# Sharing PSUM banks, splitting the first loads, and turning x by DMA in a fused attention and SoLU kernel

## The chip, the cores and the metric

The kernel runs on one core of a Trainium2 chip. The core has a matrix engine (TensorE, in the profile PE, with its weight loads shown apart as PEld), a vector engine (VectorE, DVE), a scalar engine (ScalarE, ACT), a general engine (GpSimd, POOL) and a queue engine (SyncE, SP) that here only issues DMAs. Matrix products are written to PSUM, which has eight banks of 2 KB in each of 128 partitions; VectorE and ScalarE read them from there. The metric is the device time of one execution in microseconds, lower is better.

## The reference, cut to what matters

Sizes: 4 batches, 8 heads, 768 tokens, head dimension 64; then 3072 tokens of 512 features through a layer with 1024 hidden units. Inputs and output are float32.

```python
scores = scale * q @ k.T                      # per batch and head, 768 x 768
keep = (key < 8) | ((0 <= query - key) & (query - key < 96))
scores = where(keep, scores - slope[head] * dist, -1e9)
x = softmax(scores) @ v                       # heads side by side: 3072 x 512
h = x @ w_in                                  # 3072 x 1024
solu = h * softmax(h)                         # over the 1024 units
ln = (solu - mean) / sqrt(var + 1e-6) * g_ln
out = ln @ w_out                              # 3072 x 512
```

Each query needs only the 95 keys before it, itself, and the 8 global keys. So a tile of 128 queries meets two blocks of 128 keys (one for the first tile of a batch).

## The kernel before, in words

Tokens go in 24 tiles of 128, six to a batch; tile n belongs to batch n // 6. The work of the whole program is a set of small tasks, and the names in brackets are those of the planner.

Once per batch, for each of four pairs of heads and for q and for k (eight units): load 384 KB (ql, tile `raw`, ten buffers), cast to 16 bits (qc, `qkn`, four buffers; POOL, in batch 0 also DVE), six transposes on PE into PSUM (qt, `pt`), copy to SBUF in token order (qo, `qkT`; ACT or DVE).

Once per tile: load v (vl, `vst`, four buffers), cast it on POOL (vc, into `vo`); in two halves of four heads: scores on PE (s, `ps`), exponential on ACT (e, `eb`), multiplication by the mask and bias on DVE (m), product with v on PE (av, `pav`). POOL copies the global keys and values to where the next tile finds them (gk, gv). DVE divides by the sum (n, `x16`), PE turns x with four transposes (xt, into another `pt`), DVE copies it out (xc, `xT`). Then the layer: h on PE, eight matmuls of 512 columns (h, `ph`), exponential on ACT (he, `e`), product on DVE (u, `u`), a DMA transpose of u issued by SP (ut, `uT`), squares on ACT (q), statistics on POOL or DVE (st, pw), eight matmuls into the output (o, `po`), scaling on ACT or DVE (os, `osb`), store (w).

Once in all: `w_in` is loaded by a DMA that POOL issues (L443); `w_out` in four loads; each of its eight blocks is scaled by g (gr, L453 and L456), PE forms their mean (gm, `pm`, L463), and DVE subtracts it (gc, eight instructions, L467). The first `po` needs all eight.

All PSUM pools hold one buffer each: `ps` two banks, `pav` two, `ph` two, `pt` one (for both kinds of transposes), `po` one (and `pm` once). So a step that writes `ph` waits until the product u of the tile before has been read out of it.

The order on every engine is fixed when the program is built. A list scheduler (class Plan) takes one task after the other; among the tasks that could start at about the same time on an engine it takes the one with the smallest due time, T * (n + DUE[what] + i * DUE[what+]), with two numbers per task kind from the table DUE. Its costs serve only to order the work. Every DMA except the load of w_in goes through SP's queue, in one order, and SP waits at each transposition or store until its source is ready; what stands behind waits too.

Of the kernel before, what the change touches and what calls it, by code (L numbers as in the profile page):

```python
# [100 lines left out]
def kernel(  # L101
# [24 lines left out]
    T = 4.34  # L126
    LAG = 7


    DUE = {  # L130
# [32 lines left out]
    with tc.manual_schedule():  # L163
# [35 lines left out]
        for h in range(H):  # L199
# [18 lines left out]
            rooms={"s": 1, "av": 1, "t": 1, "h": 1, "o": 1, "vst": 4, "raw": 10,  # L218
                   "qkn": 4, "eb": 4, "x16": 2, "xT": 3, "e": 3, "u": 5, "ut": 5, "uT": LAG + 1,
# [20 lines left out]

        raws, qkn, pts, qkT = {}, {}, {}, {}

        def load_pair(b, w, pr):
            t = sb.tile([P, 2, NA * D], FP32, name="raw", bufs=10)
            nc.sync.dma_start(  # L245
                out=t, in_=(q, k)[w][b, 2 * pr : 2 * pr + 2].rearrange(
                    "m (p a) d -> p m (a d)", a=NA))
            raws[b, w, pr] = t

        def cast_pair(b, w, pr, eng):  # L250
            t = sb.tile([P, NA, 2, D], FP16, name="qkn", bufs=4)
            ENG[eng](out=t.rearrange("p a m d -> p m a d"),  # L252
                     in_=raws.pop((b, w, pr)).rearrange("p m (a d) -> p m a d", d=D))
            qkn[b, w, pr] = t

        def turn_pair(b, w, pr):
            pt = pts[b, w, pr] = psum.tile([P, NA, P], FP16, name="pt", tag="t")
            src = qkn.pop((b, w, pr))
            for a in range(NA):
                nc.tensor.transpose(  # L260
                    out=pt[:, a, :], in_=src[:, a].rearrange("p m d -> p (m d)"),
                    identity=ident)

        def order_pair(b, w, pr, eng):
            if b not in qkT:
                qkT[b] = sb.tile([P, 2 * NP, S], FP16, name="qkT")
            dst = qkT[b][:, w * NP + pr, :].rearrange("p (t a) -> p t a", a=NA)
            ENG[eng](out=dst, in_=pts.pop((b, w, pr)).rearrange("p a t -> p t a"))  # L268
# [9 lines left out]
        def scores(n, half):  # L278
            b, a = divmod(n, NA)
            nb = 2 if a else 1  # L280
            ps = pss[n, half] = psum.tile([P, 2, 2, 2, P], FP32, name="ps", tag="s")
# [50 lines left out]
        def norm(n):  # L332
# [4 lines left out]
            x16 = sb.tile([P, 2, 4, D], FP16, name="x16")  # L337
# [5 lines left out]
        def turn_x(n):  # L343
            x16 = x16s.pop(n).rearrange("p g i d -> p (g i d)")
            pt = xps[n] = psum.tile([P, NCC, P], FP16, name="pt", tag="t")
            for c in range(NCC):
                nc.tensor.transpose(out=pt[:, c, :], in_=x16[:, ts(c, P)], identity=ident)  # L347

        def copy_x(n, eng):
            xTs[n] = sb.tile([P, NCC, P], FP16, name="xT", bufs=3)  # L350
            ENG[eng](out=xTs[n], in_=xps.pop(n))
# [62 lines left out]
        def ffn_out(n):  # L414
            uT = uTs.pop(n)
            po = pos[n] = psum.tile([P, D_MODEL], FP32, name="po", tag="o")
            for c in range(NFC):
                nc.tensor.matmul(out=po, lhsT=uT[:, c, :], rhs=gw_sb[:, c, :],  # L418
# [4 lines left out]
        def scale_out(n, eng):  # L423
            osb = osbs[n] = sb.tile([P, D_MODEL], FP32, name="osb", bufs=3)
            g, i = place[n]
            rs = rss[g][:, i : i + 1]
            if eng == sc:
                nc.scalar.activation(out=osb, in_=pos.pop(n), func=AF.Copy, scale=rs)  # L428
            else:
                nc.vector.tensor_scalar(out=osb, in0=pos.pop(n), scalar1=rs,  # L430
                                        scalar2=None, op0=ALU.mult)

        def store(n):
            nc.sync.dma_start(out=out[ts(n, P), :], in_=osbs.pop(n))
# [25 lines left out]
        def gw_mean():  # L460
            pms.append(psum.tile([P, D_MODEL], FP32, name="pm", tag="o"))
# [10 lines left out]
        def due(what, n, i=0):  # L472

            return T * (n + DUE[what] + i * DUE.get(what + "+", 0.0))

# [4 lines left out]
        for b in range(B):  # L480
            for i, (w, pr) in enumerate(PAIRS):
                x = (b, w, pr)
                k_ = str(min(b, 2))
                for what, engs, emit, kw in (
                    ("ql", {"SP": 0.5}, lambda e, x=x: load_pair(*x),
                     dict(takes=("raw",), load=1.08)),
                    ("qc", {gp: 0.86, ve: 0.6} if b == 0 else {gp: 0.86},
                     lambda e, x=x: cast_pair(*x, e),
# [111 lines left out]
```

## Time and profile before

| | us |
|---|---|
| median of 3 runs | 170.19 (169.99 to 170.49) |
| the profiled execution's own time | 169.84 |
| its span on the core | 168.1 |
| ACT busy | 127.3 (76%) |
| DVE busy | 118.4 (70%) |
| POOL busy | 73.8 (44%) |
| moved by DMA | 34.85 MB, 207 GB/s over the span |

The span runs from the first to the last instruction that the profiler saw on the core; 1.74 us of the execution's own time lie outside it. A row of the timeline gives start, length, engine, line of the kernel, operation, output and inputs; in brackets how long the engine had been idle and what released it. A row of the chain of waits gives start, length and what the end hung on there. In the stages (windows) each engine has its busy time in that stretch, and "DMA share" is the mean share of the 16 DMA engines that had a packet under way, which may pass 1 where packets overlap.

### The profile page before, as it was taken

The numbers are of one execution on the slowest core, as the hardware profiler recorded it, in microseconds if no ns is written. First come the engines' busy times: TensorE is split into PE (matmuls) and PEld (weight loads), VectorE is DVE, ScalarE is ACT, GpSimd is POOL, SyncE is SP. The second block draws the span as 40 slices with busy tenths as digits, with TensorE's granted clock in tenths as the row PEclk, the third lists the DMA queues.
The fourth block names the chain that finished last, engine by engine and source line by source line (L and its number), as shares of the span: only waits on it lengthen the run. The fifth ranks groups of instructions, "written<-read, shape, count | busy, mean of one in ns | idle before, by whom it ended". The sixth has DMA issues, their size and how long they took to land.

```text
span 168.1 us, 3666 instructions
## 1 busy us (share of the span) xinstructions
PE 142.3 (85%) x1384; PEld 78.7 (47%) x1384; DVE 118.4 (70%) x221; ACT 127.3 (76%) x201; POOL 73.8 (44%) x154
## 2 busy tenths in 40 slices
PE   0346479878799999999999999999999999998670
PEld 0334253455465565555545455555454555543220
DVE  1355066799998968887898778987899888744300
ACT  3955585988898978999878887879787977667511
POOL 6410116576983878636775475730404133011100
PEclk9999999999999999999999999999999999999998
DMA  5999999499999999999999999834534336545841
GB/s 177 314 314 209 349 322 346 97 278 281 189 263 312 264 359 219 226 272 226 245 304 268 260 210 257 185 96 125 127 80 113 96 95 125 125 125 125 95 161 62
DMA packets 65138, 34.85 MB, mean 207 GB/s; under 512 B 52320, under 2 KB 60512, under 8 KB 65120
## 3 DMA queue, kind: packets, MB, share of 16 engines
q1 hardware_dynamic: 64592, 33.57, 81.4%
q0 software_dynamic: 528, 1.05, 3.3%
q8 instruction: 11, 0.18, 0.5%
q14 instruction: 7, 0.06, 0.1%
HBM read 23.07 MB, written 6.29 MB: 175 GB/s over the span
## 4 chain that ended last, share of the span: by engine, by line
PE 44%; DMA 26%; SPq 16%; POOL 6%; issue 4%; DVE 2%; ACT 1%; POOLq 0%; ACTq 0%
PE ph L361 16%; PE po L418 14%; DMA raw<-in_k_dram 10%; DMA vst<-in_v_dram 6%; SPq L229 6%; SPq L245 6%; PE ps L287 5%; DMA uT<-u 5%; PE pav L325 5%; DMA raw<-in_q_dram 4%; SPq L447 3%; POOL qkn L252 3%; PE pt L260 2%; PE pt L347 2%; POOL vo L234 2%
## 5 line engine op out<-in xcount | busy, mean ns | idle before, releaser
L361 PE MATMUL ph<-w_in_sb,xT 128*128 128x512 f16 x192 | 47.1, 390 | 0.9 <-DVE u L385 0.9
L418 PE MATMUL po<-gw_sb,uT 128*128 128x512 f16 x192 | 45.3, 379 | 2.7 <-ACT osb L428 1.6
L298 ACT ACTIVATE eb<-ps 128x1024 f16<-128x1024 f32 x40 | 40.7, 1018 | 1.2 <-PE ps L287 0.7
L312 DVE TENSOR_TENSOR eb<-eb,mask 128x1024 f16<-128x1024 f16 (+1 forms) x48 | 32.8, 693 | 6.1 <-ACT eb L302 4.0
L385 DVE SCALAR_TENSOR_TENSOR u<-e,ph 128x1024 f16<-128x1024 f16 x24 | 29.2, 1216 | 8.2 <-ACT e L381 6.4
L381 ACT ACTIVATE e<-ph 128x1024 f16<-128x1024 f32 x24 | 24.6, 1024 | 11.2 <-PE ph L361 11.0
L260 PE MATMUL pt<-ident,qkn 128*128 128x128 f16 x192 | 18.4, 241 | 12.7 <-DVE qkn L252 5.3
L395 ACT ACTIVATE sq<-u 128x1024 f16<-128x1024 f16 x24 | 25.4, 1059 | 4.6 <-DVE u L385 4.6
L418 PEld LDWEIGHTS <-uT 128*128 128x128 f16 x192 | 17.6, 98 | 21.5 <-issue 2.2
L252 POOL CAST qkn<-raw 128x768 f16<-128x768 f32 x25 | 21.0, 840 | 14.7 <-DMA raw<-in_q_dram 8.6
L361 PEld LDWEIGHTS <-xT 128*128 128x128 f16 x192 | 17.8, 99 | 20.5 <-issue 3.2
L234 POOL CAST vo<-vst 128x512 f16<-128x512 f32 x24 | 16.5, 691 | 19.6 <-DMA vst<-in_v_dram 19.2
L287 PE MATMUL ps<-qkT 64*128 64x128 f16 x352 | 20.4, 230 | 4.9 <-ACT eb L298 1.9
L260 PEld LDWEIGHTS <-qkn 128*128 128x128 f16 x192 | 14.0, 107 | 16.4 <-issue 7.4
L428 ACT ACTIVATE osb<-po,rs 128x512 f32<-128x512 f32 x16 | 11.0, 684 | 11.1 <-PE po L418 8.3
L268 ACT COPY qkT<-pt 128x768 f16<-128x768 f16 x19 | 15.2, 801 | 5.4 <-PE pt L260 5.2
L287 PEld LDWEIGHTS <-qkT 64*128 64x128 f16 x352 | 11.3, 98 | 16.9 <-issue 11.1
L340 DVE TENSOR_TENSOR x<-pav,rl 128x512 f16<-128x512 f32 x24 | 16.6, 691 | 0.8
L325 PE MATMUL pav<-vo,eb 128*128 128x65 f16 x352 | 16.7, 196 | 0.2 <-POOL vo L234 0.2
L268 DVE COPY qkT<-pt 128x768 f16<-128x768 f16 x13 | 12.4, 955 | 5.8 <-PE pt L260 5.8
L412 POOL TENSOR_TENSOR rs<-vs,nhalf 128x2 f32<-128x2 f32 (+1 forms) x13 | 8.9, 685 | 14.9 <-DVE vs L407 14.5
L325 PEld LDWEIGHTS <-eb 128*128 128x128 f16 x352 | 13.1, 99 | 3.1 <-issue 0.8
(48 smaller groups left out, 111.3 us busy)
## 6 DMA issues: line engine op xcount, KB each, us to landing
raw<-in_q_dram SPq DMA_DIRECT2D x16, 384.0 KB, 5.5
raw<-in_k_dram SPq DMA_DIRECT2D x16, 384.0 KB, 5.2
vst<-in_v_dram SPq DMA_DIRECT2D x24, 256.0 KB, 5.7
out_dram<-osb SPq DMA_DIRECT2D x24, 256.0 KB, 2.7
w_out<-in_moe_w_out_dram SPq DMA_DIRECT2D x4, 512.0 KB, 10.7
w_in_sb<-in_moe_w_in_dram POOLq DMA_DIRECT2D x1, 1024.0 KB, 11.7
uT<-u SPq DMA_TRANSPOSE x24, 3.7
g_sb<-in_moe_g_ln_dram SPq DMA_DIRECT2D x1, 4.0 KB, 7.8
```

The source lines that it names most:

```text
L252: ENG[eng](out=t.rearrange("p a m d -> p m a d"), in_=raws.pop((b, w, pr)).rearrange("p m (a d) -> p m a d", d=D))
L260: nc.tensor.transpose(out=pt[:, a, :], in_=src[:, a].rearrange("p m d -> p (m d)"), identity=ident)
L268: ENG[eng](out=dst, in_=pts.pop((b, w, pr)).rearrange("p a t -> p t a"))
L287: nc.tensor.matmul(out=ps[:, m, slot, blk, :], lhsT=qkT[b][r, NP + pr, ts(a - blk, P)], rhs=qkT[b][r, pr, ts(a, P)], start=True, stop=True)
L298: nc.scalar.activation(out=eb.rearrange("p m s b f -> p (m s b f)"), in_=ps.rearrange("p m s b f -> p (m s b f)"), func=AF.Exp, scale=inv_ ...
L312: nc.vector.tensor_tensor(out=eb.rearrange(pat), in0=eb.rearrange(pat), in1=mk.rearrange(pat if n % NA else "p m s f -> p (m s f)"), op=AL ...
L325: nc.tensor.matmul(out=pav[:, half, ds(i * (D + 1), D + 1)], lhsT=eb[:, m, slot, blk, :], rhs=vo[:, b % 2, a - blk, 4 * half + i, :], star ...
L361: nc.tensor.matmul(out=ph[:, ds(fh * 512, 512)], lhsT=xT[:, j, :], rhs=w_in_sb[:, j, ds(fh * 512, 512)], start=(j == 0), stop=(j == NCC - 1))
L381: nc.scalar.activation(out=es[n], in_=phs[n], func=AF.Exp, accum_out=acc)
L385: nc.vector.scalar_tensor_tensor(out=us[n], in0=es.pop(n), scalar=1.0, in1=phs.pop(n), op0=ALU.mult, op1=ALU.mult, accum_out=sums(n, 1))
L395: nc.scalar.activation(out=sq, in_=us[n], func=AF.Square, scale=D_FF ** -0.5, accum_out=sums(n, 2))
L418: nc.tensor.matmul(out=po, lhsT=uT[:, c, :], rhs=gw_sb[:, c, :], start=(c == 0), stop=(c == NFC - 1))
```

## The change

- **PSUM.** `ps`, `pav` and `ph` share one pool of three buffers of two banks ("big"); `pt` (both kinds), `po` and `pm` share one of two single banks ("one"). Eight banks, as before.
- **First batch.** Its eight q and k units become sixteen, each with three tiles of tokens (0 to 2, then 3 to 5): 192 KB a load, three transposes, half a cast and half a copy. Scores of tiles 0 to 2 need only the first part.
- **x by DMA.** For tiles 10 to 23 the four PE transposes and DVE's copy are replaced by one DMA transpose that SP issues, 128 KB in SBUF. `x16` has three buffers in place of two, `xT` four in place of three.
- **Last output.** `po` of tile 23 is computed, scaled and stored in two halves of 256 columns.
- **Order.** T, the table DUE and the formula of due times are new (the formula has two more terms, for the first batch and for the last tiles), and the planner's costs of some PE steps are smaller. This moves nearly every instruction.

```diff
-    T = 4.34
+    T = 5.993
...
-            rooms={"s": 1, "av": 1, "t": 1, "h": 1, "o": 1, "vst": 4, "raw": 10,
-                   "qkn": 4, "eb": 4, "x16": 2, "xT": 3, "e": 3, "u": 5, "ut": 5, "uT": LAG + 1,
+            rooms={"big": 3, "one": 2, "vst": 4, "raw": 10,
+                   "qkn": 4, "eb": 4, "x16": 3, "xT": 4, "e": 3, "u": 5, "ut": 5, "uT": LAG + 1,
...
+        PARTS = {b: [(0, NA)] for b in range(1, B)}
+        PARTS[0] = [(0, NA // 2), (NA // 2, NA - NA // 2)]
...
-        def load_pair(b, w, pr):
-            t = sb.tile([P, 2, NA * D], FP32, name="raw", bufs=10)
+        def load_pair(b, a0, na, w, pr):
+            t = sb.tile([P, 2, na * D], FP32, name="raw", bufs=10)
...
-            pt = pts[b, w, pr] = psum.tile([P, NA, P], FP16, name="pt", tag="t")
+            pt = pts[b, a0, w, pr] = psum.tile([P, na, P], FP16, name="pt", tag="one", bufs=2)
...
-            ps = pss[n, half] = psum.tile([P, 2, 2, 2, P], FP32, name="ps", tag="s")
+            ps = pss[n, half] = psum.tile([P, 2, 2, 2, P], FP32, name="ps", tag="big", bufs=3)
...
-                pavs[n] = psum.tile([P, 2, 512], FP32, name="pav", tag="av")
+                pavs[n] = psum.tile([P, 2, 512], FP32, name="pav", tag="big", bufs=3)
...
+        XD = 10
+
+        def turn_x_dma(n):
+            xTs[n] = sb.tile([P, NCC, P], FP16, name="xT", bufs=4)
+            nc.sync.dma_start_transpose(
+                out=xTs[n], in_=x16s.pop(n).rearrange("p g i d -> p (g i d)"))
...
-            ph = phs[n] = psum.tile([P, D_FF], FP32, name="ph", tag="h")
+            ph = phs[n] = psum.tile([P, D_FF], FP32, name="ph", tag="big", bufs=3)
...
+        CUT = {NT - 1: 2}
+
+        def ffn_out(n, i):
+            w = D_MODEL // CUT.get(n, 1)
+            po = pos[n, i] = psum.tile([P, w], FP32, name="po", tag="one", bufs=2)
...
-            return T * (n + DUE[what] + i * DUE.get(what + "+", 0.0))
+            return T * (n + DUE[what] + i * DUE.get(what + "+", 0.0)
+                        + max(0.0, 1 - n / NA) * DUE.get(what + "*", 0.0)
+                        + max(0.0, (n - NT + NA + 1) / NA) * DUE.get(what + ">", 0.0))
...
+            if n >= XD:
+                add(("xd", n), {"SP": 0.5}, lambda e, n=n: turn_x_dma(n), n,
+                    after=[("n", n)], takes=("xT",), frees=("x16",), load=0.65)
+            else:
...
-            add(("w", n), {"SP": 0.5}, lambda e, n=n: store(n), n,
-                after=[("os", n)], frees=("osb",), load=0.75)
+                add(("w", *x), {"SP": 0.5}, lambda e, x=x: store(*x), n,
+                    after=[("os", *x)], frees=("osb",), load=0.75 / cut)
```

What this does to the order is shown at three places. In these rows stand the line, the operation, output and inputs with buffer numbers, and the output's shape.

**The start, on ACT.** First before, from the exponentials of the scores of tile 0's second half (`eb1`, of 512 columns) to the first of the layer (`e`, from `ph`) and the first squares.

```order
L302 ACTIVATE eb1_257<-ps_252 128x512
L298 ACTIVATE eb2_271<-ps_260 128x1024
L453 ACTIVATE gw_sb_71<-w_out32_69,g_sb_70 128x512
L298 ACTIVATE eb2_300<-ps_284 128x1024
L453 ACTIVATE gw_sb_71<-w_out32_69,g_sb_70 128x512
L298 ACTIVATE eb2_333<-ps_311 128x1024
L453 ACTIVATE gw_sb_71<-w_out32_69,g_sb_70 128x512
L381 ACTIVATE e_351,st_350<-ph_323 128x1024
L453 ACTIVATE gw_sb_71<-w_out32_69,g_sb_70 128x512 x2
L298 ACTIVATE eb2_374<-ps_340 128x1024
```

Now, from the fifth exponential of batch 0's full-width scores to the first scaling of w_out.

```order
L312 ACTIVATE eb2_399<-ps_348 128x1024
L312 ACTIVATE eb2_416<-ps_401 128x1024
L312 ACTIVATE eb2_463<-ps_444 128x1024
L312 ACTIVATE eb2_472<-ps_454 128x1024
L312 ACTIVATE eb2_500<-ps_489 128x1024
L312 ACTIVATE eb2_525<-ps_502 128x1024
L404 ACTIVATE e_554,st_553<-ph_534 128x1024
L404 ACTIVATE e_583,st_553<-ph_556 128x1024
L282 COPY qkT_594<-pt_596 128x768
L418 ACTIVATE sq_617,st_553<-u_571 128x1024
L404 ACTIVATE e_643,st_642<-ph_603 128x1024
L482 ACTIVATE gw_sb_71<-w_out32_69,g_sb_70 128x512 x4
```

The scores of all six tiles of batch 0 now stand ahead of the first `ph`, where six of the twelve halves did; the scaling of w_out, which stood around the exponential of the first `ph`, stands behind that of the third. In PE's order the first `po` followed four `ph` and five turns of x; it now follows six of each, with the same q and k transposes (sixteen units of six; eight of them now as sixteen of three), scores and products with v, and `pm`, on either side.

**The load of w_in, on POOL.** Before, from the last fill of a constant.

```order
L211 MEMSET meanw_127 128x128
L252 CAST qkn_156<-raw_133 128x2x6x64
L443 DMA w_in_sb_68<-in_moe_w_in_dram 128x4x1024
L234 CAST vo_67<-vst_231 128x8x64
L272 COPY qkT_152<-qkT_152 128x4x8 x2
```

Now (the rows ahead of these are seven more casts of 3 x 64 columns behind the same fill).

```order
L266 CAST qkn_236<-raw_163 128x2x3x64
L286 COPY qkT_155<-qkT_155 128x4x8
L245 CAST vo_67<-vst_184 128x8x64
L286 COPY qkT_155<-qkT_155 128x4x8
L266 CAST qkn_338<-raw_242 128x2x3x64
L266 CAST qkn_344<-raw_252 128x2x3x64
L472 DMA w_in_sb_68<-in_moe_w_in_dram 128x4x1024
```

Where the load stood behind one cast, it now stands behind ten half casts, a cast of v and two copies of global keys, which wait for the scores of tiles 1 and 2.

**The middle, on SP.** Now, about the first loads of the last batch (`raw`); before, this stretch held loads, `uT` and stores alone.

```order
L240 DMA vst_1483<-in_v_dram 128x8x64
L369 DMA_TRANSPOSE xT_1504<-x16_1500 128x4x128
L414 DMA_TRANSPOSE uT_1510<-u_1391 128x8x128
L463 DMA out_0_dram<-osb_1532 128x512
L259 DMA raw_1542<-in_k_dram 128x2x384
L259 DMA raw_1581<-in_q_dram 128x2x384
L369 DMA_TRANSPOSE xT_1605<-x16_1585 128x4x128
L259 DMA raw_1611<-in_k_dram 128x2x384
L463 DMA out_0_dram<-osb_1623 128x512
```

Each `xT` waits for its tile's division by the sum and stands ahead of loads that nothing else holds back.

More of the change, by code (lines that the diff above doesn't have):

```diff
@@ L336, in norm @@
             nc.vector.reciprocal(out=rl, in_=pav[:, :, :, D])
-            x16 = sb.tile([P, 2, 4, D], FP16, name="x16")
+            x16 = sb.tile([P, 2, 4, D], FP16, name="x16", bufs=3)
             rl_b = bass.AP(tensor=rl.tensor, offset=rl.offset,
@@ L460, in gw_mean @@
         def gw_mean():
-            pms.append(psum.tile([P, D_MODEL], FP32, name="pm", tag="o"))
+            pms.append(psum.tile([P, D_MODEL], FP32, name="pm", tag="one", bufs=2))
             for j in range(NFC):
@@ L535 @@
             add(("u", n), {ve: 1.26}, lambda e, n=n: ffn_u(n), n,
-                after=[("he", n)], takes=("u", "ut"), frees=("h", "e"))
+                after=[("he", n)], takes=("u", "ut"), frees=("big", "e"))
             add(("ut", n), {"SP": 0.5}, lambda e, n=n: turn_u(n), n, after=[("u", n)],
@@ L560 @@
             add(("gc", j), {ve: 0.74}, lambda e, j=j: gw_centre(j), 0, j,
-                after=["gm"], frees=("o",) if j == NFC - 1 else ())
+                after=["gm"], frees=("one",) if j == NFC - 1 else ())
         add("gm", {"PE": 1.75}, lambda e: gw_mean(), 0,
-            after=[("gr", j) for j in range(NFC)], takes=("o",))
+            after=[("gr", j) for j in range(NFC)], takes=("one",))
         plan.run()
```

131 lines of the change are left out of this document (73 added, 58 removed), and 23 rows, old and new, of the table DUE.

## The prediction

> **What bounds the kernel now.** I read the page's summary first, then the stages.
>
> ```profile
> span 168.1 us, 3666 instructions
> PE 142.3 (85%) x1384; PEld 78.7 (47%) x1384; DVE 118.4 (70%) x221; ACT 127.3 (76%) x201; POOL 73.8 (44%) x154
> ...
> 2.00:13.00 11.00, 3.62 (x28) 2.67 (x28) 4.31 (x8) 6.45 (x20) 4.69 (x14) 1.00 1.05 312
> 13.00:24.00 11.00, 6.63 (x66) 4.74 (x65) 4.39 (x9) 6.83 (x9) 0.82 (x2) 1.00 1.10 302
> 24.00:50.00 26.00, 22.58 (x253) 13.34 (x253) 22.76 (x41) 22.26 (x34) 17.70 (x29) 1.00 0.98 242
> 60.00:100.00 40.00, 39.59 (x410) 21.71 (x409) 32.74 (x56) 34.07 (x53) 25.50 (x48) 1.00 1.16 257
> 117.50:137.50 20.00, 20.00 (x199) 10.31 (x198) 17.64 (x35) 15.98 (x25) 5.65 (x17) 1.00 0.43 107
> 152.00:168.10 16.10, 9.28 (x40) 3.71 (x39) 2.48 (x10) 6.08 (x10) 1.10 (x2) 0.96 0.52 116
> ```
>
> Each stage has PE, PEld, DVE, ACT and POOL busy, then granted clock, DMA share and GB/s. From 60 us to about 148 PE hardly rests (39.59 of 40, then 20 of 20): that stage is PE's. Ahead of it PE has little to do while DMA is full (share 1.05 and 1.10), and behind it PE waits for one tile's chain. DMA stays full until 100 us (1.16) and is half empty later.
>
> Busy time hides how fast PE could go, since matmuls overlap in it. The chain of waits shows the pace, as each piece there ends where the next begins.
>
> ```profile
> 58.35 0.59 PE pav L325 x16
> 58.94 0.33 PE pt L260 x6
> 59.27 1.73 PE ph L361 x8
> 61.00 0.22 PE pt L347 x4
> 61.22 0.33 PE ps L287 x8
> ...
> 62.23 1.73 PE po L418 x8
> ...
> 64.29 0.44 PE pt L260 x6
> ...
> 67.14 0.33 PE pt L347 x4
> ```
>
> So PE's work at full pace is: 24 `ph` and 24 `po` of 1.73 (83.0), `pm` at the same price (1.7), 352 score matmuls at 0.33 per eight (14.5), 352 of `pav` at 0.59 per sixteen (13.0), 32 q and k transposes of six at 0.36, between 0.33 and 0.44 (11.5), 24 turns of x at 0.24, between 0.22 and 0.33 (5.8). Together **129.5 us**.
>
> I keep a ledger: PE's *debt* at an instruction is its start less the work that stands ahead of it in PE's order. Three rows of PE's timeline give it, and the chain's end the rest.
>
> ```profile
> 49.84 1.89 PE L418 MATMUL po<-gw_sb,uT 128*128 128x512 f16 x8
> ...
> 151.99 1.89 PE L361 MATMUL ph<-w_in_sb,xT 128*128 128x512 f16 x8 [0.74 <-DVE u L385]
> ...
> 162.12 1.90 PE L418 MATMUL po<-gw_sb,uT 128*128 128x512 f16 x8 [1.14 <-DMA uT<-u]
> 164.20 0.69 ACT L428 ACTIVATE osb<-po,rs 128x512 f32<-128x512 f32 x1 [2.44 <-PE po L418]
> ```
>
> - First `po`, 49.84: ahead stand 4 `ph`, `pm`, 16 q and k units, 100 score matmuls, 88 of `pav`, 5 turns of x, 22.9 us. Debt 26.9.
> - Last `ph`, 151.99: all but itself and four `po` is done, 120.9. Debt 31.1, so 4.2 more in 100 us.
> - Last `po`, 162.12: 127.8 is done. Debt 34.3, another 3.2.
> - From there to the end, 168.1 - 162.12 = 6.0.
>
> The span is 127.8 + 26.9 + 4.2 + 3.2 + 6.0 = 168.1. The change is priced term by term.
>
> **Work.** Fourteen turns of x leave PE: 14 x 0.24 = 3.4 (3.1 to 4.6 by the two rows). The halves of the first batch and of the last `po` have the same columns, so nothing is added. The last `po` now has 124.4 ahead of it, **-3.4**. DVE also loses fourteen copies, but it is not the bound in the saturated stage (32.74 of 40 us), and this is worth nothing by itself. ACT (34.07 of 40) stays below PE too.
>
> **Debt at the first `po`.** Ahead of it now stand six `ph` and six turns in place of four and five: 26.6 us. When it starts follows from three things. First, w_in (two groups of ACT, the timelines of POOL, ACT and PE, and the page's list of DMA issues, whose last number is the time to landing):
>
> ```profile
> L298 ACT ACTIVATE eb<-ps 128x1024 f16<-128x1024 f32 x40 | 40.7, 1018 | 1.2 <-PE ps L287 0.7
> ...
> L302 ACT ACTIVATE eb<-ps 128x512 f16<-128x512 f32 x8 | 4.8, 594 | 0.8 <-PE ps L287 0.8
> ...
> 8.12 1.09 POOL L443 DMA_DIRECT2D w_in_sb<-in_moe_w_in_dram  x1
> 8.62 0.78 ACT L268 COPY qkT<-pt 128x768 f16<-128x768 f16 x1
> ...
> w_in_sb<-in_moe_w_in_dram POOLq DMA_DIRECT2D x1, 1024.0 KB, 11.7
> ...
> 24.93 3.60 PE L361 MATMUL ph<-w_in_sb,xT 128*128 128x512 f16 x8
> ...
> 37.10 1.90 PE L361 MATMUL ph<-w_in_sb,xT 128*128 128x512 f16 x8
> ```
>
> The load was issued at 8.12 and landed 11.7 later, well ahead of the first `ph` at 24.93. Now POOL reaches it only after a copy of global keys that needs both halves of tile 2's scores. ACT is free of masks at 8.62; then come an exponential of 0.6, one of 1.0, three half copies (about 0.45 each, from 0.8 for a whole one) and 0.6 again until the bank for the last of those scores is free: 12.2. With those scores, the copy, a cast of v and two half casts POOL issues at 15.0 (14 to 17), and w_in lands at **26.7**. The exponentials of all twelve halves of batch 0 end by about 24 on ACT, so the first `ph` waits for w_in and starts 1.8 *later* than before.
>
> Second, that `ph` takes 3.6 instead of 1.9, as before: matmuls behind a thin stretch run at half pace here. [...]
>
> Third, the way to `po`. ACT has, from the end of the first `ph` at 30.3, four exponentials of the layer, a copy of q or k, two squares and five scalings of w_out before `pm` can run, about 10.6 us by these rows, and waits about 1 for PE's second and third `ph`:
>
> ```profile
> L381 ACT ACTIVATE e<-ph 128x1024 f16<-128x1024 f32 x24 | 24.6, 1024 | 11.2 <-PE ph L361 11.0
> L395 ACT ACTIVATE sq<-u 128x1024 f16<-128x1024 f16 x24 | 25.4, 1059 | 4.6 <-DVE u L385 4.6
> L453 ACT ACTIVATE gw_sb<-w_out,g_sb 128x512 f16<-128x512 f32 x5 | 3.5, 711 | 0.0
> L467 DVE SCALAR_TENSOR_TENSOR gw_sb<-w_out,g_sb,pm 128x512 f16<-128x512 f32 x8 | 5.8, 738 | 0.0
> ```
>
> (Mean ns stand behind the busy time.) `pm` starts at 42.0 and ends at 43.7; eight subtractions take 5.6, beside which PE has 5 us of other work. First `po` at **49.3**, debt 22.7, against 26.9: **-4.2**. So PE does 3.7 us more work in 0.5 less time, because batch 0's attention fills the time in which w_in is under way. Bounds: w_in at 24 gives -6.9; the old debt gives 0.
>
> **Middle.** Of the 4.2 that the debt grew, the last two `ph` waited 0.2 and 0.74 for the one `ph` buffer; three shared buffers end that. I keep the other 3.2, since the same loads arrive through the same full DMA: **-1.0**. Bounds: 0 left, -4.2; and all x transposes exposed, in the rivals. The x transposes take at least 3 us to land, as `uT` shows below, and the order leaves two tiles between a division and its `ph`, over 5 us. What else SP's order queues behind an `xT` is loads, with four to ten buffers ahead.
>
> **Tail.** Before, the last `ph`, its exponential, product and transpose led to the last `po` in 10.1. The transpose in the chain, and all of them from issue to landing:
>
> ```profile
> 156.84 5.24 DMA uT<-u
> ...
> DMA to landing us min/median/max: 3.0/3.7/7.0
> ```
>
> With a median landing of 3.7 in place of 5.24 that would be 8.6. PE now has the last `ph` and four `po`, 8.65, in the same time, and the second `po` bank removes its waits for ACT. I take 9.6, so the debt grows by 1.0 rather than 3.2: **-2.2**. The end: two half `po` 1.9, half a scaling (0.5 of 0.69), and the store's 168.1 - 164.89 = 3.2, with hops 5.7 for 6.0: **-0.3**.
>
> **Sum.** 124.4 + 22.7 + 3.2 + 1.0 + 5.7 = 157.0 of span. The profiled execution took 169.84, 1.74 outside its span: **158.7 us**, 11.1 (6.5%) less than its 169.84, which itself lies 0.35 under the median of 170.19.
>
> **Rivals.**
>
> *The x transposes cost DMA time.* From 117.5 to 137.5 DMA carried four `uT` and four stores with a share of 0.43, 8.6 us, 2.15 a pair. A 256 KB store at the 312 GB/s of the first stage is 0.84, so `uT` is 1.3 and an `xT`, half of it, 0.65. Eight of them fall ahead of the last batch's loads, where the share was 1.16; if all are exposed, +5.2: **163.9**. For it: DMA was full there. Against it: PE was never short of data in that stage. [...]
>
> *The start gains nothing.* The late w_in and the scalings behind the third `ph` move the first `po` so far that the debt is 26.9 again: **162.9**. It would show as a first `po` at 53.5.
>
> *The start gains all.* w_in at 24 and no growth of the debt in the middle: 158.7 - 2.7 - 3.2 = **152.8**.
>
> *SP's queue, the slower side.* SP works in order, and an `xT` that waits, or is slow to issue, holds loads.
>
> ```profile
> 74.62 5.06 SPq L391 DMA_TRANSPOSE uT<-u  x1
> ...
> 113.42 1.23 SPq L391 DMA_TRANSPOSE uT<-u  x1
> ```
>
> In the full stage a `uT` once held SP for 5.06, in the idle one 1.23. If an `xT` does so and PE runs dry, each costs 3.8. Three would make it 170.1, no change; from the fourth on the kernel is **slower, 173.9**. Against it: in those 5 us PE had no gap.
>
> *The change does not do what it says.* If one pool of three buffers makes `ph`, `ps` and `pav` wait for each other where separate ones did not, PE's debt grows by what the buffers save, and only the work leaves: 166.4.
>
> **How the numbers follow.** Forecast 0.50 (155.5 to 162); the start gains all 0.13; DMA time 0.12; no gain at the start 0.12; shared buffers 0.04; no change by a mix of these 0.03; SP's queue 0.06. The unknowns reach from 152.5 (all of the better ends) to 166.5 (both worse ones in part), which leaves out less than 2 in 10. About 0.3%, 0.5 us, is what a measurement of this kernel can tell from no change. Faster 0.91, same 0.03, slower 0.06.
>
> **What would show it.** In the profile after: w_in issued at 14 to 17 and the first `ph` at 25 to 28.5 with 3.6; first `po` at 47 to 52; between it and the last `ph` PE at 95% or more; the last `ph` at about 141.5, the last `po` ten later; no copies L374 after tile 9. The prediction is wrong if PE shows gaps behind DMA or POOL casts between 55 and 120, if `ph` waits for exponentials of scores, or if the last `xT` come so late that the four last `ph` do not follow each other.

## The result, and the profile after

| | before | after |
|---|---|---|
| median of 4 runs each, us | 170.25 (169.99 to 170.49) | 157.06 (156.52 to 157.49) |
| ratio, 95% interval | | 0.922 (0.919 to 0.926) |
| the profiled execution: own time, span | 169.84, 168.1 | 157.49, 155.7 |

Faster by 7.8%. The forecast was 158.7, so 1.6 too high, inside its range. Executions of one kernel differ by up to 3.3% (155.17 to 160.3 us): the ratios below leave out those more than 1.5% above its fastest, the medians do not, and four profiles (x back on PE, private banks, the three small loads, the kernel before with x by DMA) are of such slower executions. The page's summary and the same six stages as before (PE, PEld, DVE, ACT, POOL busy, granted clock, DMA share, GB/s):

```profile
span 155.7 us, 3671 instructions
PE 136.4 (88%) x1336; PEld 77.0 (49%) x1336; DVE 118.3 (76%) x216; ACT 123.3 (79%) x200; POOL 76.8 (49%) x163
...
2.00:13.00 11.00, 6.63 (x48) 3.37 (x48) 6.53 (x15) 7.04 (x22) 6.75 (x20) 1.00 1.01 283
13.00:24.00 11.00, 8.49 (x122) 6.69 (x120) 9.92 (x18) 7.64 (x11) 6.76 (x13) 1.00 1.08 209
24.00:50.00 26.00, 20.86 (x190) 11.76 (x190) 21.41 (x37) 18.95 (x31) 11.69 (x22) 0.93 1.18 282
60.00:100.00 40.00, 39.29 (x436) 22.78 (x434) 33.44 (x59) 35.53 (x55) 25.00 (x48) 1.00 1.09 253
106.00:126.00 20.00, 20.00 (x207) 10.66 (x204) 16.20 (x29) 17.45 (x27) 8.90 (x22) 1.00 1.24 223
140.00:155.70 15.70, 12.18 (x64) 6.04 (x62) 5.47 (x19) 9.14 (x18) 1.79 (x3) 0.99 0.64 168
```

Ahead of 24 us PE is busy 15.1 where it was 10.3. From 60 us on it is as full as before. What is new is DMA: full (1.24) even from 106 to 126; before, its share was 0.43 from 117.5 on. The instructions on which the ledger rests, from the timelines of POOL, PE and DVE:

```profile
16.79 0.95 POOL L472 DMA_DIRECT2D w_in_sb<-in_moe_w_in_dram  x1
...
28.82 3.24 PE L384 MATMUL ph<-w_in_sb,xT 128*128 128x512 f16 x8 [2.44 <-DMA w_in_sb<-in_moe_w_in_dram]
...
42.40 1.90 PE L492 MATMUL pm<-gw_sb,meanw 128*128 128x512 f16 x8
...
45.78 5.34 DVE L496 SCALAR_TENSOR_TENSOR gw_sb<-w_out,g_sb,pm 128x512 f16<-128x512 f32 x8
...
51.05 0.49 PE L274 MATMUL pt<-ident,qkn 128*128 128x128 f16 x6 [1.21 <-POOL vo L245]
51.38 1.89 PE L444 MATMUL po<-gw_sb,uT 128*128 128x512 f16 x8
...
141.48 1.89 PE L384 MATMUL ph<-w_in_sb,xT 128*128 128x512 f16 x8
143.21 9.02 PE L444 MATMUL po<-gw_sb,uT 128*128 128x512 f16 x48
```

The last row is four whole `po` and the two halves without a gap, so the last tile's `po` starts at 143.21 + 4 x 1.73 = 150.1. The debt, start less work ahead (26.6, 115.7 and 124.4 us, as in the prediction), with a second profile of the same kernel from another set of runs beside it:

| debt at | before | forecast | after | after, second profile |
|---|---|---|---|---|
| first `po` | 26.9 | 22.7 | 24.8 | 20.9 |
| last `ph` | 31.1 | 25.9 | 25.8 | 23.5 |
| last `po` | 34.3 | 26.9 | 25.7 | 23.5 |
| from there to the end | 6.0 | 5.7 | 5.6 | 5.5 |
| span | 168.1 | 157.0 | 155.7 | 153.4 |

### The profile page after: what moved, and what is told of

The parts are those of the page before. It is cut to its first block, busy times and chain, and to the rows that moved or that the text cites. A ratio compares the mean times of both kernels' runs of the same rounds, so it can differ in the third digit from the quotient of the medians.

```text
span 155.7 us, 3671 instructions
## 1 busy us (share of the span) xinstructions
PE 136.4 (88%) x1336; PEld 77.0 (49%) x1336; DVE 118.3 (76%) x216; ACT 123.3 (79%) x200; POOL 76.8 (49%) x163
## 3 DMA queue, kind: packets, MB, share of 16 engines
q1 hardware_dynamic: 74528, 35.40, 99.3%
## 4 chain that ended last, share of the span: by engine, by line
PE 69%; DMA 14%; ACT 4%; DVE 3%; POOL 3%; issue 3%; SPq 2%; POOLq 0%; DVEq 0%; ACTq 0%
PE po L444 27%; PE ph L384 26%; DMA w_in_sb<-in_moe_w_in_dram 8%; PE ps L301 6%; PE pav L339 5%; PE pt L274 4%; DMA raw<-in_q_dram 3%; DMA raw<-in_k_dram 3%; ACT eb L312 2%; SPq L259 2%; POOL qkn L266 2%; ACT sq L418 1%; DVE gw_sb L485 1%; PE pt L361 1%; DVE u L408 1%
## 5 line engine op out<-in xcount | busy, mean ns | idle before, releaser
L444 PE MATMUL po<-gw_sb,uT 128*128 128x512 f16 (+1 forms) x200 | 44.9, 371 | 0.0
L326 DVE TENSOR_TENSOR eb<-eb,mask 128x1024 f16<-128x1024 f16 (+1 forms) x48 | 34.9, 743 | 5.1 <-ACT eb L312 4.5
L266 POOL CAST qkn<-raw 128x768 f16<-128x768 f32 (+1 forms) x34 | 26.6, 784 | 10.3 <-DMA raw<-in_q_dram 6.8
L274 PEld LDWEIGHTS <-qkn 128*128 128x128 f16 x192 | 12.8, 104 | 14.1 <-POOL qkn L266 5.4
L301 PE MATMUL ps<-qkT 64*128 64x128 f16 x352 | 17.9, 232 | 1.6 <-ACT eb L312 1.3
L245 POOL CAST vo<-vst 128x512 f16<-128x512 f32 x24 | 14.6, 616 | 8.4 <-DMA vst<-in_v_dram 8.3
L282 DVE COPY qkT<-pt 128x384 f16<-128x384 f16 (+1 forms) x20 | 15.1, 755 | 4.7 <-PE pt L274 4.5
L249 POOL COPY vo<-vo 8x520 f16<-8x520 f16 x16 | 10.1, 630 | 17.1 <-PE pav L339 16.9
L339 PEld LDWEIGHTS <-eb 128*128 128x128 f16 x352 | 15.2, 101 | 5.3 <-DVE eb L326 0.5
L282 ACT COPY qkT<-pt 128x768 f16<-128x768 f16 (+1 forms) x20 | 14.0, 704 | 1.4 <-PE pt L274 1.1
```

Of the source, the lines that this page charges most:

```text
L266: ENG[eng](out=t.rearrange("p a m d -> p m a d"), in_=raws.pop((b, a0, w, pr)).rearrange("p m (a d) -> p m a d", d=D))
L274: nc.tensor.transpose(out=pt[:, a, :], in_=src[:, a].rearrange("p m d -> p (m d)"), identity=ident)
L282: ENG[eng](out=dst, in_=pts.pop((b, a0, w, pr)).rearrange("p a t -> p t a"))
L301: nc.tensor.matmul(out=ps[:, m, slot, blk, :], lhsT=qkT[b][r, NP + pr, ts(a - blk, P)], rhs=qkT[b][r, pr, ts(a, P)], start=True, stop=True)
L326: nc.vector.tensor_tensor(out=eb.rearrange(pat), in0=eb.rearrange(pat), in1=mk.rearrange(pat if n % NA else "p m s f -> p (m s f)"), op=AL ...
L339: nc.tensor.matmul(out=pav[:, half, ds(i * (D + 1), D + 1)], lhsT=eb[:, m, slot, blk, :], rhs=vo[:, b % 2, a - blk, 4 * half + i, :], star ...
```

## The experiments

Theory: the four gains of the forecast are real and separate (x off PE, a denser start, shared buffers in the middle, a second `po` bank in the tail), and w_in's landing limits the start. The rivals: the gain hangs on one part alone, or the x transposes by DMA cost as much as they save. All runs had three rounds against the kernel before on the same chip; ratios have 95% intervals.

**x of tiles 10 and up back on PE, all else kept** (transposes and copy stand where SP issued the DMA):

```diff
         def turn_x_dma(n):
-            xTs[n] = sb.tile([P, NCC, P], FP16, name="xT", bufs=4)
-            nc.sync.dma_start_transpose(
-                out=xTs[n], in_=x16s.pop(n).rearrange("p g i d -> p (g i d)"))
+            turn_x(n)
+            copy_x(n, ve)
```

> The changed kernel with its order kept, but x of tiles 10 to 23 turned by PE (four transposes) and copied by DVE at the place where the DMA transpose was issued. If PE's work sets the pace from tile 10 on, 14 turns of 0.24 come back: 157.1 + 3.4 = 160.5 us (up to 162 if PE waits for the division right behind the products). Rival, the DMA transposes cost as much as they save because DMA is full: 155 to 157 us, and the DMA share of the queue falls by some 9 points.

162.66 us, ratio 0.950 (0.944 to 0.956), against 0.922: the transposes by DMA are worth 2.8% of 170.2, about 4.8 us (3.6 to 6.0). The theory's direction holds; the time is 0.7 above its bound of 162, and the size above the forecast's 3.4. The rest is in PE's timeline of this kernel, whose first row is of use further down:

```profile
27.05 3.59 PE L383 MATMUL ph<-w_in_sb,xT 128*128 128x512 f16 x8 [1.04 <-DMA w_in_sb<-in_moe_w_in_dram]
...
75.98 0.42 PE L339 MATMUL pav<-vo,eb 128*128 128x65 f16 x8 [0.54 <-DVE eb L326]
...
79.43 1.89 PE L443 MATMUL po<-gw_sb,uT 128*128 128x512 f16 x8 [0.63 <-DVE xT L373]
...
101.04 0.40 PE L301 MATMUL ps<-qkT 64*128 64x128 f16 x8 [1.08 <-DVE u L407]
```

PE waits for DVE, which has fourteen copies more: for a bank that the copy holds, and for products behind it. From 55 us on its waits for DVE come to 3.3 us; the profile after has none there. The order was planned for x by DMA, so part of this may be the order's: a table made for x by PE was not run.

**w_in issued earlier, all else kept**, behind POOL's cast of the eighth first-part unit:

```diff
         def cast_pair(b, a0, na, w, pr, eng):
...
             qkn[b, a0, w, pr] = t
+            if (b, a0, w, pr) == (0, 0, 1, 3):
+                load_w_in()
```

> The changed kernel with everything in its order but the issue of the w_in load, which moves on POOL to right behind the last cast of the first half of k, about 11.5 us in place of 16.8. If w_in alone holds the first ph (PE idle 2.4 us before it) and nothing behind it is later for another reason, w_in lands at 23.5, the first ph starts at 26.4 and the end comes 2.4 us earlier: 154.7 us. Rival, the scaling and centring of w_out hold the first po: first ph at 26.4 but first po still near 51.4, and 157 us.

159.53 us, ratio 0.936 (0.930 to 0.942): slower than after, as neither expected. Timelines of POOL and PE:

```profile
10.60 0.97 POOL L474 DMA_DIRECT2D w_in_sb<-in_moe_w_in_dram  x1
...
21.14 1.04 PE L341 MATMUL pav<-vo,eb 128*128 128x65 f16 x16 [2.30 <-POOL vo L245]
...
29.66 1.89 PE L386 MATMUL ph<-w_in_sb,xT 128*128 128x512 f16 x8
...
52.86 1.89 PE L446 MATMUL po<-gw_sb,uT 128*128 128x512 f16 x8
```

w_in landed 6.6 us sooner (10.6 + 11.6 = 22.2), but `pav` now waited for the casts of v, PE reached the first `ph` only at 29.7, and the first `po` came 1.5 later. In POOL's timeline two of these casts waited 4.53 and 1.74 us for their loads; in the profile after, none in that stretch did (over the span the casts of v waited 14.0 us for loads here, 8.3 there). So w_in, put ahead, put the loads of v behind.

**Private banks for the new table** (the planner orders the work anew from the same table, with one buffer for each of `ps`, `pav`, `ph`, `pt` and `po`):

```diff
-            rooms={"big": 3, "one": 2, "vst": 4, "raw": 10,
+            rooms={"s": 1, "av": 1, "t": 1, "h": 1, "o": 1, "vst": 4, "raw": 10,
...
-            ph = phs[n] = psum.tile([P, D_FF], FP32, name="ph", tag="big", bufs=3)
+            ph = phs[n] = psum.tile([P, D_FF], FP32, name="ph", tag="h", bufs=1)
```

> The changed kernel with private PSUM buffers again (ps, pav, ph, pt, po one each, in the planner too, so the order is planned anew from the same table). If the shared pools are what stopped the debt from growing in the middle (4.2 before, 1.0 after) and in the tail (3.2 before, 0 after), 157.1 + 3.2 + 3.2 = 163.5 us. Rival, the order of the start and x by DMA made the gain and the pools nothing: 157 to 158 us.

187.23 us (183.06 to 188.53; too uneven for a ratio), 10% *slower* than before. PE's waits, with us in total, times and the longest:

```profile
PE pt L274 <- DVE qkT L282: 6.3, 7, 1.4
PE pt L274 <- ACT qkT L282: 6.1, 10, 1.3
PE ph L384 <- DVE u L408: 4.1, 7, 0.8
...
PE pav L339 <- DVE x L354: 3.5, 5, 1.0
```

Each is a product that waits until its one buffer has been read. The direction is the theory's, the size neither's: this table does not fit private banks.

**The first batch's loads whole again** (`PARTS[0] = [(0, NA)]`; the planner orders anew):

> The changed kernel with the first batch of q and k in whole units again (planned anew). Scores of tile 2 then need loads of 13 us in place of about 10, so w_in is issued some 3 us later and the first ph and all behind it start 3 us later: 160 us. Rival, the start has slack elsewhere: first po within 1 us of 51.4 and 157 to 158 us.

163.83 us, ratio 0.960 (0.953 to 0.968). The start did not suffer: w_in was issued at 14.9, and the first `ph` came sooner than after.

```profile
25.71 1.89 PE L384 MATMUL ph<-w_in_sb,xT 128*128 128x512 f16 x8
...
49.01 1.89 PE L444 MATMUL po<-gw_sb,uT 128*128 128x512 f16 x8
...
50.00:75.00 25.00, 20.89 (x256) 12.74 (x254) 21.75 (x37) 20.02 (x30) 19.70 (x34) 1.00 1.19 263
```

The loss is largest at 50 to 75 (PE 20.9 of 25, where the profiles after have 23.4 and 24.5), in an order that the planner made anew. So this run says nothing certain of the split itself; what the split is worth is left open.

**The changed kernel again**, beside the next three:

> The changed kernel again, unedited, beside the three below on their chip. Expected: 157.1 us (156.5 to 157.6), 0.922 of the kernel before; w_in issued at about 16.8 and landed some 12 us later, first po at about 51.4. It is the bar for the other three, since the last set ran on a chip on which the kernel before spread from 169.6 to 172.9.

156.72 us (155.17 to 160.3), ratio 0.915 (0.899 to 0.931). Its profile is the second one of the table above, and it shows what a few us at the start are worth:

```profile
15.97 0.95 POOL L472 DMA_DIRECT2D w_in_sb<-in_moe_w_in_dram  x1
...
26.63 1.90 PE L384 MATMUL ph<-w_in_sb,xT 128*128 128x512 f16 x8 [1.13 <-DMA w_in_sb<-in_moe_w_in_dram]
...
47.55 1.89 PE L444 MATMUL po<-gw_sb,uT 128*128 128x512 f16 x8
...
89.33 0.51 PE L274 MATMUL pt<-ident,qkn 128*128 128x128 f16 x6 [0.30 <-POOL qkn L266]
...
97.19 1.90 PE L384 MATMUL ph<-w_in_sb,xT 128*128 128x512 f16 x8 [0.95 <-DMA xT<-x]
```

w_in took 10.6 us to land and not 12.0, so the first `po` came 3.8 sooner; yet the last `ph` came only 2.3 sooner (139.22). PE then waits for data at 89 and 97, where the first profile has no such wait: an earlier PE meets loads and transposes that are not earlier by as much.

**The second batch's first q and k load behind the next v load** (issued at 18.05 and 19.74, where the second profile has 16.57 and 17.70; the expectation had meant 21.7):

```diff
+        held = []
+        def load_pair(b, a0, na, w, pr, again=False):
+            if b == 1 and pr == 0 and not again:
+                held.append((b, a0, na, w, pr))
+                return
...
         def load_v(n):
...
+            while held:
+                load_pair(*held.pop(0), again=True)
```

> The first q and k load of the second batch (two of 384 KB, issued at 17.5 and 18.5 in the changed kernel, in the midst of w_in's 12 us) are issued behind the next v load instead, at about 21.7; all else keeps its order. Theory: the start lost the 2.1 us of the forecast because w_in shares 16 full DMA engines with loads that nobody needs yet. At about 280 GB/s the 0.75 MB are 2.7 us; by about half of that w_in lands sooner (27.0 to 27.5 instead of 28.8), the first ph starts there, the first po about 1 us sooner (50.2), and the kernel ends at 156.0 (155.5 to 156.5). Rival: between the first ph and the first po something else sets the pace (in the changed kernel a transpose waits 1.21 us for POOL's v copy at 51.05, and POOL there waits for the second batch's loads); then w_in may land sooner, but the first po stays at 51.4 or comes later, and the time is 157 to 158.5.

155.7 us (155.25 to 156.26), ratio 0.917 (0.907 to 0.926); not told apart from the changed kernel's 0.915 in the same set. w_in landed at 26.0, 0.6 sooner than in the second profile, and the first `po` came at 47.20 for 47.55; a transpose ahead of it waited 1.43 for the cast of loads that had been held, where it had waited 1.21 for POOL. By the last `ph` (140.30) it was behind. Inconclusive in time: 155.7 is what the theory gave, but the changed kernel beside it reached 155.2. The rows fit the rival better.

**w_in in two transfers**, each of half the contraction:

```diff
-            nc.gpsimd.dma_start(out=w_in_sb, in_=moe_w_in.rearrange("(j p) f -> p j f", p=P))
+            src = moe_w_in.rearrange("(j p) f -> p j f", p=P)
+            for i in range(2):
+                nc.gpsimd.dma_start(out=w_in_sb[i], in_=src[:, 2 * i : 2 * i + 2])
```

> w_in as two transfers of half the contraction each, one behind the other at the same place of POOL; ph's matmuls are in that order already. Theory (w_in's landing holds the start): the first half lands some 6 us ahead of the second, so the first ph starts at about 26.4, behind the last attention product before it, and only its last four matmuls wait for the second half at about 29; PE wins about 1 us of the 2.44 it idles and the cold clock is used up in it: first po 50.4, kernel 156.2 (155.5 to 156.8). Rival: the second issue costs POOL another 0.95 us ahead of its v copies, which hold PE's next products at 20 to 26, and nothing or less than nothing is won: 157 to 158.5.

156.54 us (154.85 to 157.8), ratio 0.917 (0.897 to 0.937): the same. The first `ph` started at 26.73 without a wait for DMA and took 1.95, and the page's clock row reads 9 tenths in every slice: the low clock that the profile after has behind its wait (0.55 from 29 to 31 us) is not in this one, so whether a wait can use it up was not shown. The first `po` came at 48.78, 1.2 later than in the second profile, as the rival had it.

**Each x transpose issued twice**, the second into a buffer that nobody reads:

```diff
+            xTd = sb.tile([P, NCC, P], FP16, name="xTd", bufs=2)
+            nc.sync.dma_start_transpose(
+                out=xTd, in_=xkeep[n].rearrange("p g i d -> p (g i d)"))
```

> Each of the 14 x transposes by DMA is issued twice, the second into a spare buffer that nobody reads. Theory of the forecast: they lie beside PE's work, so a second set costs PE nothing although it adds 14 times 1.2 us to SP and raises the queue's share of the 16 engines by what an x transpose really takes (0.65 us each as forecast: 9 us; 0.8 as the profile after against the one with x by PE has it: 11.5); time 157 to 158. Rival: the x transposes already cost on the path through full engines and SP's order (the forecast's first rival, +0.65 us each for 14), and a second set then adds 7 to 10 us: 164 to 167.

170.98 us, ratio 1.007 (1.003 to 1.012): 14.3 more than the changed kernel in the same set (14.4 by the ratio, against 0.922), 1.0 for each, more than the rival had. The forecast's cover is gone at once. SP's timeline of this kernel, then PE's:

```profile
82.74 1.96 SPq L370 DMA_TRANSPOSE xT<-x  x1
84.75 2.56 SPq L373 DMA_TRANSPOSE xTd<-x  x1
87.36 1.30 SPq L418 DMA_TRANSPOSE uT<-u  x1
...
89.33 0.44 SPq L259 DMA_DIRECT2D raw<-in_k_dram  x1
...
94.66 0.82 PE L274 MATMUL pt<-ident,qkn 128*128 128x128 f16 x6 [3.00 <-POOL qkn L266]
...
144.53 2.45 PE L448 MATMUL po<-gw_sb,uT 128*128 128x512 f16 x8 [3.72 <-DMA uT<-u]
```

The load of k that stands at 89.33 here was issued at 84.19 in the second profile after. Three extra transposes stand ahead of it by then, and PE waits 3.00 us for the cast of what they held up.

**The same hold of SP's queue with next to no bytes:** behind each x transpose three loads of 256 bytes.

```diff
+            for i in range(3):
+                tiny = sb.tile([1, D], FP32, name=f"tiny{i}", bufs=4)
+                nc.sync.dma_start(out=tiny, in_=q[0, 0, 0:1, :])
```

> Behind each of the 14 x transposes SP issues three loads of 256 bytes that nobody reads, instead of a second transpose: at 0.42 us each SP's queue is held as long (1.26 us) as by an x transpose (1.22 to 1.27), and the 16 engines get next to nothing. It tells which resource made the second set cost 14 us. Theory A: the 16 engines; then SP's time alone costs little, 157 to 158.5. Theory B: SP's order, since what stands behind a transpose there (loads of q, k and v, stores) is issued later by its issue time; then most of the 14 us come back: 166 to 171. Between the two, both have a part.

166.8 us, ratio 0.978 (0.973 to 0.984), 9.5 above the changed kernel's 0.922. The page's queue row of the run before (transposes twice), then of this one:

```profile
q1 hardware_dynamic: 82144, 37.24, 98.0%
```

```profile
q1 hardware_dynamic: 74612, 35.42, 90.6%
```

The 16 engines were given 98.0% x 169.4 = 166.0 us there and 90.6% x 169.0 = 153.1 here, no more than the changed kernel's 99.3% x 155.7 = 154.6. So time on SP's in-order queue costs by itself: the three loads hold it for 1.02 us at the median, 16.3 in all, for 9.5. The second transposes held it for 1.27 at the median, 21.7 in all; at the same rate that is 12.6 of their 14.4. The rest may be the engines' part; that is argued from two runs, not shown. Nor is it told apart whether it is the issue or some fixed cost of a transfer in the queue.

**The kernel before with x by DMA alone** (tiles 10 and up, issued where DVE's copy stood; table, banks and buffers are before's):

```diff
+        XD = 10
         def turn_x(n):
+            if n >= XD:
+                return
...
         def copy_x(n, eng):
             xTs[n] = sb.tile([P, NCC, P], FP16, name="xT", bufs=3)
+            if n >= XD:
+                nc.sync.dma_start_transpose(
+                    out=xTs[n], in_=x16s.pop(n).rearrange("p g i d -> p (g i d)"))
+                return
```

> The kernel before with one part of the change alone: x of tiles 10 and up is transposed by DMA, issued where the copy on VectorE stood; table, pools and order are before's. Theory (the ledger of PE's work): 14 times 0.24 us of PE go and before's queue has room (81% of 16 engines' time), so 170.2 - 3.4 = 166.8 (165.5 to 168.5). Rival: in the old order PE is paced in the middle by private banks and by their readers, not by its work, and a transpose that lands 2.5 us or more after its issue holds ph of the tile as long as before: 169 to 172.

178.78 us, ratio 1.040 (1.034 to 1.046): *slower*, and beyond the rival. SP's timeline, then PE's:

```profile
89.08 3.02 SPq L399 DMA_TRANSPOSE uT<-u  x1
92.20 4.04 SPq L229 DMA_DIRECT2D vst<-in_v_dram  x2
96.34 1.40 SPq L356 DMA_TRANSPOSE xT<-x  x1
...
95.50 0.62 PE L325 MATMUL pav<-vo,eb 128*128 128x65 f16 x8
100.19 3.60 PE L369 MATMUL ph<-w_in_sb,xT 128*128 128x512 f16 x8 [4.07 <-DMA xT<-x]
```

PE waits 4.07 us for the transpose of tile 11. That tile's division had ended at 87.24, so there was time; but in SP's order the transpose stood behind one of u, whose product ended only at 92.02, and two loads of v that held SP for 4.04, and it was issued at 96.34. PE waited for x three times in all, 6.7 us. The kernel differs from the changed one in order, banks and in the buffers of `x16` and `xT`; which of them hides the transposes there is not told apart.

**The kernel before with the shared pools alone** (order, loads and x as before):

```diff
-            ph = phs[n] = psum.tile([P, D_FF], FP32, name="ph", tag="h")
+            ph = phs[n] = psum.tile([P, D_FF], FP32, name="ph", tag="big", bufs=3)
...
-            po = pos[n] = psum.tile([P, D_MODEL], FP32, name="po", tag="o")
+            po = pos[n] = psum.tile([P, D_MODEL], FP32, name="po", tag="one", bufs=2)
```

> The kernel before with the other part alone: the shared pools of 3 double and 2 single banks, with before's table, order, whole loads and PE's x transposes. With the run of the new order on private banks (187) it completes the square of order and banks. Theory: the two belong together; with an order that was made for private banks the pools change little, since products rotate through the banks in the order of issue: 168 to 172. Rival: the pools are the gain and the order serves them only a little: 160 to 165.

166.91 us, ratio 0.978 (0.972 to 0.983), between the two. PE's timeline:

```profile
50.59 1.89 PE L418 MATMUL po<-gw_sb,uT 128*128 128x512 f16 x8
...
151.01 1.89 PE L361 MATMUL ph<-w_in_sb,xT 128*128 128x512 f16 x8
152.73 5.63 PE L418 MATMUL po<-gw_sb,uT 128*128 128x512 f16 x24
158.98 1.90 PE L418 MATMUL po<-gw_sb,uT 128*128 128x512 f16 x8 [0.62 <-DMA uT<-u]
```

The first `po` comes 0.8 later than before, the last `ph` 1.0 sooner, the last `po` 3.1 sooner. So between first `po` and last `ph` the debt grows by 2.4 in place of 4.2, and in the tail by 1.1 in place of 3.2: for the buffers the forecast had 1.0 and 2.2 less, and the runs have 1.8 and 2.1.

**Fewer x transposes with the later loads:** the run with the held loads, and x of tiles 10 to 13 back on PE.

```diff
         def turn_x_dma(n):
+            if n < 14:
+                turn_x(n)
+                copy_x(n, ve)
+                return
```

> The kernel with the second batch's first loads behind the v load (155.7 on the last chip), and x of tiles 10 to 13 back on PE (DMA from 14 on). Theory: what an earlier start wins is given back at 90 to 98 us, where the full DMA lands xT and q, k late (PE 8.5 to 8.9 of 10 us there, against 9.8 in the first profile after); four x transposes less take about 3 us from the 16 engines ahead of that place, the waits there go (1.3 us), and PE pays 4 times 0.24: 0.3 to 0.5 less than without, 155.2 (154.5 to 156). Rival: a tile's x on PE costs what the run with all 14 on PE cost, 0.35 us each, and the DMA waits stay: 157 to 157.5.

158.61 us (156.64 to 160.71; too uneven for a ratio). The stage from 85 to 100 in the first profile after, in the second, and in this kernel with two rows of its timeline:

```profile
85.00:100.00 15.00, 14.81 (x172) 8.69 (x169) 12.52 (x21) 13.15 (x20) 10.10 (x21) 1.00 1.20 264
```

```profile
85.00:100.00 15.00, 13.56 (x152) 7.68 (x151) 11.40 (x18) 12.35 (x19) 9.29 (x18) 1.00 1.14 290
```

```profile
85.00:100.00 15.00, 14.50 (x171) 8.76 (x170) 13.57 (x24) 12.78 (x19) 9.99 (x20) 1.00 0.92 234
...
73.46 0.42 PE L346 MATMUL pav<-vo,eb 128*128 128x65 f16 x8 [0.57 <-DVE eb L333]
...
76.91 1.89 PE L455 MATMUL po<-gw_sb,uT 128*128 128x512 f16 x8 [0.63 <-DVE xT L385]
```

DMA's share fell to 0.92 and the waits for xT and for the casts at 85 to 100 are gone, as the theory had it. But the copies are back on DVE, and PE waits for them 10 us earlier. None of the variants is shown to beat the changed kernel.

## Why the prediction was right, and where its sizes were off

The runs give a chain from before to after:

| step | ratio so far | this step, us of 170.2 | forecast |
|---|---|---|---|
| shared pools in the old order | 0.978 | -3.8 | middle and tail, -3.2 |
| new order, split first batch, last output in halves | 0.950 | -4.7 | first `po` and end, -4.5 |
| x of tiles 10 and up by DMA | 0.922 | -4.8 | work, -3.4 |

The first step's interval is 1 us to either side, that of the others 1 to 1.4, and the ratios are of three sets of runs. The second step stands beside the terms that its edits were to bring; it was not measured stage by stage. And the split holds for this path only: taken first, x by DMA costs 6.8.

- **Work (-3.4): mis-sized, -4.8.** 14 x 0.24 us left PE, as priced. The step that failed is that DVE's copies are "worth nothing by itself": with x on PE in the new order, PE waited for them and for what stood behind them.
- **First `po` (-4.2): right on its first half, wrong on its second, and its size not fixed by the kernel.** -2.1 in the first profile, -6.0 in the second. w_in was issued at 16.79 and 15.97 where 15.0 was forecast, and took 12.0 and 10.6 to land where 11.7 was. Yet in the first profile `pm` started at 42.40, only 0.4 behind the forecast, since ACT's way from the first `ph` to `pm` took 10.3 and not 11.7. The step that failed stands behind `pm`: the forecast let the eight subtractions begin where `pm` ends, but DVE's order has two products u ahead of them. They began 1.6 later, at 45.78 (1.2 later in the second profile), and ended at 51.12; the transpose that stands ahead of `po` on PE ended just behind, after a wait for POOL. With 1.9 for the first `ph` in place of the 3.6 that was taken over from before, the first `po` forecast at 49.3 would be 47.6, and the second profile, where it took 1.90, has 47.55. That is partly luck: there ACT's way was about as much shorter as DVE's was longer.
- **Pace of the first `ph` (3.6): not set by the order.** It took 3.24 in the first profile and 1.90 in the second, where w_in landed at 26.6 (forecast 26.7). The forecast took the 3.6 over from before, where that `ph` took 3.60 at a granted clock of 1.00 (24.9 to 28.5 us); in the first profile the clock was 0.56 (28.8 to 32.1 us). No run shows what sets this pace, and the length of the wait does not tell the cases apart: 2.44 us idle gave 3.24, 1.13 gave 1.90, 1.04, with x back on PE, gave 3.59, and none, before, 3.60.
- **Middle (3.2 of growth kept): mis-sized, 1.0 in the first profile, 2.6 in the second.** The prediction took start and middle as separate. By the profiles they are not: the later PE gets to the stage from 85 to 100, the less it waits there for xT and the casts of q and k (14.81 and 13.56 busy of 15 with a first `po` at 51.38 and 47.55; 13.54 with the held loads, at 47.20). That is read from three profiles; no run moved the start alone. So 2.1 too little at the start and 2.2 too much in the middle cancelled in the first profile: that the sum came so near is in part luck. By the prediction's own sign, gaps behind DMA or POOL's casts between 55 and 120, the first profile has none and the second 1.25 us.
- **Tail (1.0 kept): mis-sized, 0.** The four `po` and two halves ran without a gap from 143.21, so the last `po` came 8.65 us behind the last `ph`, where 9.6 had been allowed for transposes that land late. The pools alone gave 2.1 of it in the old order.
- **End: 5.6 for 5.7.**
- **The x transposes are hidden: right for this order, and with hardly any margin.** The forecast's argument, that what stands behind an `xT` on SP is loads "with four to ten buffers ahead", does not hold: a second set cost 1.0 us each, and the same hold of SP without the bytes 0.7. The rivals of DMA time and of SP's queue named mechanisms that the runs show. They did not decide: in the two profiles of the changed kernel PE waits 0 and 0.95 us for an x transpose; in the old order, with its banks and buffers, 6.7, and there the same transposes cost 6.8 us.
- **The change does what it says.** The shared buffers hardly make the products wait for each other: in the first profile no `ph` or `pav` waits for a bank, and `ps` waits for exponentials 1.3 us in all, where before it waited 2.6. Private ones under the new table do.

## What to carry to other kernels

Moving work from a full engine to an idle one pays only if the order has room for it, on the queue that takes it too: the same fourteen DMA transposes gave 4.8 us in a kernel planned for them and cost 6.8 in one that was not, where they stood behind waiting issues on SP. Before relying on "hidden", double the hidden thing once; here it turned from free to 1 us each, which tells how near the next limit is. Follow the whole chain to a milestone on every engine: here two products that stood ahead on DVE were left out. And where one stage waits for loads, terms of a ledger that lie ahead of that stage need not add to those in it: check by a second profile whether a gain at the start is still there at the end.

## What the runs showed of the hardware that was not expected

An x transpose of 128 KB holds SP's queue about as long as one of u with twice the bytes: 1.22 us against 1.30 at the median. The runs that added such holds, by a second set and by the small loads, were 14.4 and 9.5 us longer; a load of 192 KB held SP for 0.4 to 0.5 us (15 of the 16 in the profile after; one took 1.97). Of the 16 engines' time an x transpose took about 0.8 us where the forecast had 0.65: with x back on PE they were given 88.0% x 162.5 = 143.0 us, so 14 x transposes took 11.6 by the profile after, and the second set another 11.4 (0.6 to 1.0 each with the second profile's 157.1 in place of 154.6).

```profile
L369 SPq DMA_TRANSPOSE xT<-x x14: 1194/1223/1650, 74.0 to 137.9; - x14
...
L414 SPq DMA_TRANSPOSE uT<-u x24: 1232/1302/2491, 34.5 to 145.8; - x24
```

(The numbers behind the count are the least, median and greatest ns, then the first and last start.) And the granted clock behind a short wait ahead of the first `ph` was not the same in three profiles: after 2.44 us in the profile after it was 0.55 from 29 to 31 us; after 1.13 in the second profile it stayed at 1.00; with x back on PE, where the wait was 1.04 and ended at 27.05, the page's slices read 6 tenths from 20.3 to 24.4 us, 7 to 28.4 and 5 to 32.5, so there it was low ahead of the wait too. PE had been busy 1.8 of the 3 us from 23 to 26 in the profile after and 1.9 with x back on PE; these figures do not tell what decided it.
